# Moving VectorE work out of a crowded stage, and score steps later, in a fused retention and feed-forward kernel

## The chip, the cores and the metric

The kernel runs on one core of a Trainium2 chip. The metric is the time of one execution on the device in microseconds (us). The profile is one recorded execution. Its span leaves out some 1.7 us that the timed execution has around it, so spans are compared with spans and times with times. The profiled execution of the kernel before took 306.74 us, less than any of the timed ones beside it, so the gain is about 0.65 us smaller by the two profiled executions than by the medians.

The profile names the engines so: PE is TensorE (matmuls), DVE is VectorE, ACT is ScalarE, POOL is GpSimd, SP is SyncE; `SPq` and `ACTq` are DMA sends issued from SyncE's and ScalarE's queues.

## The reference, cut to what matters

```python
# q, k, v: [8 batches, 8 heads, 576 positions, 64], float32
scores = q @ k.T / sqrt(64)                       # per batch and head
ret    = scores * where(i >= j, gamma[h] ** (i - j), 0)
x      = (ret @ v)  -> [4608 tokens, 512]         # heads side by side
h      = x @ w_in                                 # 512 x 2048
g      = gelu_tanh(h)
out    = g @ w_out                                # 2048 x 512, float32
```

The decay mask can be factored over chunks of 128 positions. The kernel therefore works out scores within a chunk and carries a scanned state from chunk to chunk.

Of the kernel before, what the change touches and what calls it, by code (L numbers as in the profile page):

```python
# [19 lines left out]
def kernel(  # L20
# [9 lines left out]
    nc = tc.nc  # L30

    B, H, S, D = q.shape
    NT, DM = out.shape
    DF = moe_w_in.shape[1]
    HP = H // 2
    NC = S // 128
# [13 lines left out]
    NTB = NT // TB  # L50
# [121 lines left out]
    for u in range(2):  # L172
# [15 lines left out]
        out=cm, in_=cm, compare_op=ALU.is_ge, fill=0.0, base=0,  # L188
# [5 lines left out]
        out=tm, in_=tm, compare_op=ALU.is_ge, fill=0.0, base=0,  # L194
# [4 lines left out]
    for h in range(H):  # L199
        u = 64 * (h % 2)  # L200
# [78 lines left out]
    def turn(b, c, copy, tag="att"):  # L279
        a = att[b]  # L280
        t = bank(tag, "tr", F16)
        n = HP if c < NC else 2
        keys = "k" if b < NQ and c < NC else "kq"
        for y, key in enumerate(keys):
            for i in range(n):
                o = (512 * c if c < NC else 0) + 128 * i
                nc.tensor.transpose(
                    t[:, 128 * (n * y + i) : 128 * (n * y + i) + 128], act_of(b, key, c)[:, o : o + 128], ident
                )
        m = len(keys)  # L290
        d, o = turned(b, c)
        copy(
            out=d[:, 0:m, o : o + n, :].rearrange("p y n t -> p y (n t)"),
            in_=t[:, 0 : 128 * n * m].rearrange("p (y x) -> p y x", y=m),
        )
# [149 lines left out]
    def ost():  # L445
        return sb.tile([128, 2, DM], F32, tag="ost", name="ost", bufs=2)
# [17 lines left out]
    HD = DM // 2  # L464
# [4 lines left out]
    def weight_sums(f, names="1324"):  # L469
        s = slice(f, f + 4)  # L470
        w = {
            "1": (W12, W11, ALU.subtract), "3": (W22, W12, ALU.subtract),
            "2": (wt["3"], W11, ALU.add), "4": (W21, wt["2"], ALU.subtract),
        }
        for o in names:
            x, y, f = w[o]
            nc.vector.tensor_tensor(out=wt[o][:, s], in0=x[:, s], in1=y[:, s], op=f)  # L477
# [35 lines left out]
    keep = {}  # L513

    def after(t, m, u):
        last = t == NTB - 1
        if u == 0 and not (last and m in (6, 7, 4)):
            return
        us = slice(u, u + 1) if last and m in (6, 7, 4) else slice(0, 2)
        def pr(tag):  # L520
            return op[tag, u].rearrange("p (u d) -> p u d", u=2)
        def add(o, a, b):
            nc.vector.tensor_tensor(out=o, in0=a, in1=b, op=ALU.add)  # L523
        def send(o, i):
            if t < B:
                nc.sync.dma_start(
                    out=out[S * t : S * t + TB, :].rearrange("(u i p) d -> p u i d", u=2, i=2)[:, :, i, :], in_=o
                )
                return
            for v in range(2):  # L530
                end(o[:, v], i, v)
        def end(o, i, v, d=slice(0, DM)):
            b = 4 * v + 2 * i
            for h, e in enumerate((nc.sync, nc.scalar)):
                r0 = S * (b + h) + M0
                e.dma_start(out=out[r0 : r0 + TL, d], in_=o[TL * h : TL * h + TL, d])
        if m == 1:
            keep["s1"] = sb.tile([128, 2, HD], F32, tag="k1", name="k1", bufs=1)
            nc.scalar.copy(out=keep["s1"], in_=pr("A"))
        elif m == 6:  # L540
            if us.start == 0:
                keep["u2"] = sb.tile([128, 2, HD], F32, tag="k2", name="k2", bufs=1)
            add(keep["u2"][:, us], keep["s1"][:, us], pr("B")[:, us])
        elif m == 7:
            if us.start == 0:
                keep["u3"] = sb.tile([128, 2, HD], F32, tag="k3", name="k3", bufs=1)
            add(keep["u3"][:, us], keep["s1"][:, us], pr("B")[:, us])
            if u == 0:
                return
            keep["o1"] = ost()  # L550
            add(keep["o1"][:, :, HD:DM], keep["u3"], pr("C"))
            if last:
                for v in range(2):
                    end(keep["o1"][:, v], 1, v, slice(HD, DM))
        elif m == 2:
            keep["o0"] = ost()
            nc.scalar.copy(out=keep["o0"][:, :, 0:HD], in_=pr("A"))  # L557
        elif m == 3:
            add(keep["o0"][:, :, HD:DM], keep["u2"], pr("C"))
            send(keep["o0"], 0)  # L560
        elif m == 4:
            if last:
                add(keep["o1"][:, u, 0:HD], keep["s1"][:, u], pr("B")[:, u])
                end(keep["o1"][:, u], 1, u, slice(0, HD))
            else:
                add(keep["o1"][:, :, 0:HD], keep["s1"], pr("B"))
                send(keep["o1"], 1)
# [25 lines left out]
    V, P, A = nc.vector, nc.gpsimd, nc.scalar  # L593
# [48 lines left out]
    def at(t, u, f):  # L642
        if t > 0 and u > 29:
            t, u = t + 1, u - 30
        events.setdefault((t, u), []).append(f)
# [11 lines left out]
    at(0, 1, lambda: (new_casts(1), new_turned(1)))  # L657
    for p in range(HP):
        at(0, 2 + p, lambda p=p: cc(1, "q", p, V))
    at(0, 27, lambda: weight_sums(0, "32"))  # L660
    at(1, 4, lambda: weight_sums(0, "1"))
    at(1, 8, lambda: weight_sums(0, "4"))
    for p in range(HP):
        at(0, (20, 21, 22, 24)[p], lambda p=p: turn_q4(1, p, A.copy))
    CU = [(0, 6), (0, 27), (0, 31), (1, 0)]
# [6 lines left out]
        at(*VU[c], lambda c=c: (av(1, c, "AB"[c] if c < 2 else "att"), inter(1, c), put(1, c), spread(1, c, A.copy)))  # L672
    for c in range(NC):
        at(*SU[c], lambda c=c: (score(1, c), state(1, c), scan(1, c)))
    at(1, 10, lambda: weight_sums(4, "32"))
    at(1, 18, lambda: weight_sums(4, "1"))
    at(1, 24, lambda: weight_sums(4, "4"))


    def scores(t, u, *xs):  # L680
        at(t, u, lambda: [score(*x) for x in xs])
# [15 lines left out]
    def values(t, u, *xs):  # L697
        at(t, u, lambda: ([av(*x) for x in xs], [inter(*x[:2]) for x in xs]))
        for n, x in enumerate(xs):
            at(t, u + 1 + n, lambda x=x: put(*x[:2]))  # L700
# [5 lines left out]
        at(k[0], k[1] + 3, go)  # L706

    def turns_of(t, u, b, c, tag):
        at(t, u, lambda: turn(b, c, V.tensor_copy, tag))

    for b, (l, k, v) in TAILS.items():
        if b == 0:
# [6 lines left out]
    for t in range(1, 7):  # L719
        b, e = t + 1, t - 3  # L720
        if t == 1:
            for c, (u, tag) in enumerate(((7, "t2"), (9, "A"), (15, "C"), (17, "hp"))):
                turns_of(t, u, b, c, tag)
            u0, u1, u2, u3 = 11, 17, 19, 25
            states(t, u0, b, 0, "B")
            scores(t, u0, (b, 0, ("t0", "t1")), (b, 1, ("t2", "A")))
        else:
            u0, u1, u2, u3 = (8, 14, 19, 25) if t == 2 else (6, 12, 17, 24)
            tail = [(e, NC, ("B", "C"))] if e >= 0 else []
            scores(t, u0, (b, 0, ("t0", "t1")), (b, 1, ("t2", "A" if t > 2 else "C")), *tail)  # L730
        states(t, u1, b, 2, "t0")
        values(t, u1, (b, 0, "t1"), (b, 1, "t2"), *([(e, NC, "B")] if e >= 0 else []))
        scores(t, u2, (b, 2, ("t1", "t2")), (b, 3, ("hp", "hp")))
        if t < 6:
            states(t, u3, b + 1, 0, "t0")
        values(t, u3, (b, 2, "t1"), (b, 3, "t2"))
# [26 lines left out]
    for t in range(NTB):  # L763
        steps = []
        if t == 0:
            tags = ("A", "B", "C", "hp")
            for i0, f0, f1 in ((0, 0, 12), (2, 0, 8), (0, 12, 16), (2, 8, 16)):
                for f in range(f0, f1):
                    steps.append(lambda f=f, i0=i0: [down_mm(0, i0 + n, f, tags[i0 + n]) for n in range(2)] and None)
                if f1 == NF:  # L770
                    steps.append(lambda i0=i0: store_pair(0, i0))
        else:
            for u in range(2 if t == 1 else 0):
                for f in (0, NH, 2, NH + 2, 4, NH + 4, 6, NH + 6):
                    def half(u=u, f=f):
                        up_half(t, u, f)
                        if f in (NH + 2, NH + 6):
                            return lambda: act_sums(t, f - NH - 2, f - NH + 2, slice(u, u + 1))
                    steps.append(half)
            for f in range(0 if t == 1 else NH):  # L780
                steps.append(lambda f=f: up(t, f))
                def hi(f=f):
                    up(t, f + NH)
                    if f % 2:
                        return lambda: act_sums(t, f - 1, f + 1)
                steps.append(hi)
            for m in (1, 6, 5, 7, 2, 3, 4):
                for u in range(2):
                    steps.append(lambda m=m, u=u: (prod(t, m, u), after(t, m, u)))
        for u, s in enumerate(steps):  # L790
            then = s()
            run(t, u)
            if callable(then):
                then()
# [31 lines left out]
```

## The kernel before: the parts that the change touches

The tokens are done in nine blocks of 512 (`t` = 0 to 8). A block has a first layer of 16 steps `up` (four matmuls and a gelu each; in blocks 0 and 1 a step is eight matmuls of half width and a gelu, in an order of their own) and a second layer. The attention of batch t+1 is laid into the steps of block t, each piece at a fixed place: `at(t, u, f)` puts the work `f` into block t after step u. Block 0 counts its steps from the start of its second layer.

From block 1 on the second layer is done with seven half-size products in place of eight (a Strassen-like scheme). It needs sums of weight quarters, made once, and sums of gelu outputs, made in every block, both on VectorE. Each product fills one PSUM bank, A, B or C, and the bank must be copied or added away before the next product that uses it:

```python
def weight_sums(f, names="1324"):                 # one 128x1024 addition each
    ...
    for o in names:
        nc.vector.tensor_tensor(out=wt[o][:, s], in0=x[:, s], in1=y[:, s], op=f)

def act_sums(t, f0, f1, us=slice(0, 2)):          # four additions on VectorE: s1, s2, in place, s4
    ...
tag = {1: "A", 2: "A", 3: "C", 4: "B", 5: "C", 6: "B", 7: "B"}[m]     # bank of product m
...
for m in (1, 6, 5, 7, 2, 3, 4):                   # order of the products, two steps each
    for u in range(2):
        steps.append(lambda m=m, u=u: (prod(t, m, u), after(t, m, u)))
```

Batch 2 is transposed on TensorE and copied out of PSUM (`turn`); later batches are transposed by DMA, and TensorE meets the result in its scores. The steps at which a batch's scores, states and values stand:

```python
def turns_of(t, u, b, c, tag):
    at(t, u, lambda: turn(b, c, V.tensor_copy, tag))        # the copy is on VectorE
...
u0, u1, u2, u3 = (8, 14, 19, 25) if t == 2 else (6, 12, 17, 24)
scores(t, u0, ...first pair of chunks...)                   # masks "ret" on VectorE
states(t, u1, b, 2, "t0")                                   # then four spreads on ScalarE, at u1+2 to u1+5
values(t, u1, ...)                                          # xT copies on ScalarE, at u1+1 and u1+2
scores(t, u2, ...second pair...)
states(t, u3, b + 1, 0, "t0")                               # four spreads, at u3+2 to u3+5
values(t, u3, ...)
```

Steps 0 to 15 of blocks 2 and later are the first layer, 16 to 29 the products. A step past 29 runs on into the next block: with u3 = 25 the fourth spread, at u3+5, stands after step 0 of the next block.

## Time and profile before

| | before |
|---|---|
| time, median of the 4 runs beside the first run of the change | 307.39 us (307.03 to 307.96) |
| span of the profiled execution | 305.0 us |
| TensorE busy | 292.2 us, 96% |
| VectorE busy, whole span | 177.4 us, 58% |
| slices of VectorE from 61 to 84 us | 9, 9, 9 tenths |
| product stages of blocks 1 and 6 start | 73.92 us, 230.41 us |
| start of the last matmul to end | 4.96 us |

TensorE bounds the kernel, so the only question is where TensorE waits, and how long. Block 1 is the exception: there VectorE has no room, and TensorE waits for it.

### The profile page before, as it was taken

Reading aid. Unit: us, or ns where it says so; the run is one execution under the profiler, and the core shown is the slowest. Engines: PE = TensorE matmul, PEld = TensorE weight load, DVE = VectorE, ACT = ScalarE, POOL = GpSimd, SP = SyncE. Lnnn points to the kernel's source line nnn. Section 1 sums busy time; section 2 is a strip of 40 time slices with the busy share of each in tenths; the row PEclk is TensorE's granted clock in tenths of the full one; section 3 lists DMA queues with packets and bytes.
Section 4 is the critical chain, followed back from the end, with each engine's and each line's share of the span. In section 5 each row is a group of like instructions: output and inputs, shape, how many; then the busy total and the mean of one; then the engine's idle time right before and its main releaser. Section 6 shows DMA issues by size and latency. Waiting matters only on the chain.

```text
span 305.0 us, 6861 instructions
## 1 busy us (share of the span) xinstructions
PE 292.2 (96%) x2747; PEld 198.4 (65%) x2747; DVE 177.4 (58%) x362; ACT 168.5 (55%) x327; POOL 120.8 (40%) x178
## 2 busy tenths in 40 slices
PE   6899999999899999999999999999999899999993
PEld 2568655788784588457845785578557754784583
DVE  6652757699962865386538653865396335342432
ACT  6666417976556583659355936493647246316600
POOL 8679114560835069204920393039757110000000
PEclk9999999999999999999999999999999999999999
DMA  8999999999999995999399959963962140103004
GB/s 210 219 331 384 384 243 222 210 256 243 215 184 225 202 259 92 199 206 284 69 218 202 263 31 232 221 150 52 236 132 55 33 156 11 26 17 122 2 0 138
DMA packets 130591, 52.87 MB, mean 173 GB/s; under 512 B 118784, under 2 KB 121344, under 8 KB 130560
## 3 DMA queue, kind: packets, MB, share of 16 engines
q1 hardware_dynamic: 128544, 48.77, 74.0%
q0 software_dynamic: 1536, 3.15, 4.5%
q10 hardware_dynamic: 480, 0.52, 0.6%
q8 instruction: 21, 0.34, 0.5%
q14 instruction: 10, 0.08, 0.1%
HBM read 36.70 MB, written 9.44 MB: 151 GB/s over the span
## 4 chain that ended last, share of the span: by engine, by line
PE 66%; DVE 13%; ACT 5%; DMA 5%; SPq 5%; POOL 3%; issue 2%; DVEq 0%; POOLq 0%
PE hp L415 28%; PE opB L508 9%; PE hp L432 6%; PE opC L508 6%; PE opA L508 5%; PE op L451 4%; DVE ret L324 4%; SPq L95 3%; DMA tt<-cq 3%; ACT gT L421 2%; PE xs L367 2%; DMA ld<-in_moe_w_in_dram 2%; PE st L317 2%; PE xs L388 2%; DVE wt L477 1%
## 5 line engine op out<-in xcount | busy, mean ns | idle before, releaser
L415 PE MATMUL hp<-xT,w_in_sb 128*128 128x512 f16 x448 | 100.6, 379 | 0.1
L421 ACT ACTIVATE gT<-hp 128x512 f16<-128x512 f32 x112 | 66.9, 598 | 50.9 <-PE hp L415 44.0
L415 PEld LDWEIGHTS <-w_in_sb 128*128 128x128 f16 x448 | 42.9, 98 | 50.0 <-issue 2.0
L508 PEld LDWEIGHTS <-gT 128*128 128x128 f16 x512 | 49.8, 98 | 9.8 <-issue 2.6
L324 DVE TENSOR_TENSOR ret<-st,cm 128x512 f16<-128x512 f32 x64 | 40.0, 682 | 9.5 <-PE st L317 8.5
L488 DVE TENSOR_TENSOR s<-gT 128x512 f16<-128x512 f16 x32 | 14.0, 438 | 49.6 <-ACT gT L421 49.6
L257 POOL TENSOR_TENSOR ck<-ld,sc 128x512 f16<-128x512 f32 x31 | 32.8, 1059 | 23.4 <-DMA ld<-in_k_dram 22.2
L508 PEld LDWEIGHTS <-s 128*128 128x128 f16 x384 | 37.2, 98 | 6.0 <-issue 0.7
L508 PE MATMUL opA<-w_out_sb,gT 128*128 128x256 f16 x256 | 31.2, 273 | 0.6 <-DVE ret L324 0.6
L508 PE MATMUL opB<-wt,gT 128*128 128x256 f16 x256 | 30.6, 273 | 1.2 <-DVE k L523 0.8
L432 PE MATMUL hp<-xT,w_in_sb 128*128 128x256 f16 x256 | 29.8, 273 | 0.3 <-POOL w_in_sb L580 0.2
L557 ACT COPY ost<-opA 128x512 f32<-128x512 f32 x8 | 4.7, 585 | 46.0 <-PE opA L508 38.6
L752 POOL COPY gate<-s 128x1 f16<-128x1 f16 x5 | 0.9, 188 | 65.9 <-DVE s L491 57.4
L257 POOL TENSOR_TENSOR cq<-ld,sc 128x512 f16<-128x512 f32 x24 | 26.3, 1097 | 1.6 <-DMA ld<-in_q_dram 1.4
L432 PEld LDWEIGHTS <-w_in_sb 128*128 128x128 f16 x256 | 24.5, 98 | 3.7 <-POOL w_in_sb L580 0.4
L438 ACT ACTIVATE gT<-hp 128x512 f16<-128x512 f32 x32 | 19.1, 597 | 7.3 <-PE hp L432 7.3
L359 ACT CAST tbd<-ws 64x256 f16<-64x256 f32 x48 | 19.3, 402 | 2.9 <-DVE ws L354 2.2
L523 DVE TENSOR_TENSOR k<-k,opB 128x512 f32<-128x512 f32 (+1 forms) x18 | 11.3, 625 | 16.2 <-PE opB L508 14.8
L405 ACT CAST xT<-xs 128x512 f16<-128x512 f32 x32 | 18.5, 583 | 2.5 <-PE xs L388 2.1
L523 DVE TENSOR_TENSOR ost<-k,opC 128x512 f32<-128x512 f32 x16 | 11.0, 687 | 14.3 <-PE opC L508 14.0
L508 PE MATMUL opC<-wt,s 128*128 128x256 f16 x128 | 15.5, 273 | 0.6 <-DVE wt L477 0.6
L244 ACT CAST cv<-ld 128x512 f16<-128x512 f32 x27 | 15.7, 616 | 0.3
(95 smaller groups left out, 366.8 us busy)
## 6 DMA issues: line engine op xcount, KB each, us to landing
ld<-in_q_dram SPq DMA_DIRECT2D x32, 256.0 KB, 5.1
ld<-in_k_dram SPq DMA_DIRECT2D x32, 256.0 KB, 5.1
ld<-in_v_dram SPq DMA_DIRECT2D x32, 256.0 KB, 5.0
out_dram<-ost SPq DMA_DIRECT2D x16, 512.0 KB, 5.0
ld<-in_moe_w_in_dram SPq DMA_DIRECT2D x16, 256.0 KB, 5.6
ld<-in_moe_w_out_dram SPq DMA_DIRECT2D x16, 256.0 KB, 6.0
lt<-in_k_dram POOLq DMA_DIRECT2D x16, 64.0 KB, 4.6
lt<-in_q_dram POOLq DMA_DIRECT2D x16, 64.0 KB, 4.5
```

Source lines behind the costliest of these rows:

```text
L244: eng.copy(out=dst, in_=raw)
L257: eng.tensor_tensor(out=dst.rearrange("p (h d) -> p h d", d=D), in0=raw.rearrange("p (h d) -> p h d", d=D), in1=sc[:, s0 : s0 + nh].unsque ...
L324: nc.vector.tensor_tensor(out=r, in0=st[hl][:, 0:w], in1=m.rearrange("p n i -> p (n i)"), op=ALU.mult)
L359: cp(out=(tbd[b % 2][r, c, :, r] if c < NC - 1 else tbt[b % 4][r, :, r]), in_=att[b]["w", c][r])
L405: nc.scalar.copy(out=xT[:, g0 : g0 + 2], in_=src)
L415: nc.tensor.matmul(hp.rearrange("p (g t) -> p g t", t=TL), w_in_sb[:, ct, 128 * fc : 128 * fc + 128], xT[:, o : o + TB // TL, ct, :], star ...
L421: nc.scalar.activation(out=gT[t][:, fc].rearrange("p i n -> p (i n)"), in_=hp, func=AF.Gelu_apprx_tanh)
L432: nc.tensor.matmul(hp[:, 256 * x : 256 * x + 256].rearrange("p (g t) -> p g t", t=TL), w_in_sb[:, ct, 128 * (f + x) : 128 * (f + x) + 128] ...
L438: nc.scalar.activation(out=gT[t][:, f : f + 2, 2 * u : 2 * u + 2, :].rearrange("p f i n -> p f (i n)"), in_=hp.rearrange("p (f n) -> p f n ...
L488: nc.vector.tensor_tensor(out=s["1"], in0=a21, in1=a22, op=ALU.add)
L508: nc.tensor.matmul(op[tag, u][:, HD * u : HD * u + HD], lhs(f), rhs[:, f], start=(new and (u == 0 or own) and f == 0), stop=(f == NH - 1), ...
L523: nc.vector.tensor_tensor(out=o, in0=a, in1=b, op=ALU.add)
```

## The change

The intent has four parts. The first takes weight sums off VectorE in block 1, where it is full, and makes six of the eight in block 0. The second gives ScalarE the copies of batch 2's transposes. The third sets the second pair's scores behind product 6 (step 19 for 17), so that the masks no longer delay the addition that frees bank B, and exchanges banks to suit; in block 3 it also moves the first scores and states by a step, and in blocks 3 to 6 it moves the second values and the next batch's first states from step 24 to 25. The fourth changes the last block's product order, so that the large output sends leave earlier.

```diff
-    at(0, 27, lambda: weight_sums(0, "32"))
-    at(1, 4, lambda: weight_sums(0, "1"))
-    at(1, 8, lambda: weight_sums(0, "4"))
+    for t, u, f, n in ((0, 21, 0, "32"), (0, 22, 4, "3"), (0, 24, 4, "2"), (0, 27, 0, "1"), (0, 28, 4, "1"),
+                       (1, 20, 0, "4"), (1, 24, 4, "4")):
+        at(t, u, lambda f=f, n=n: weight_sums(f, n))
...
-    at(1, 10, lambda: weight_sums(4, "32"))
-    at(1, 18, lambda: weight_sums(4, "1"))
-    at(1, 24, lambda: weight_sums(4, "4"))
...
-        at(t, u, lambda: turn(b, c, V.tensor_copy, tag))
+        at(t, u, lambda: turn(b, c, A.copy, tag))
...
-            u0, u1, u2, u3 = (8, 14, 19, 25) if t == 2 else (6, 12, 17, 24)
+            u0, u1, u2, u3 = (8, 14, 19, 25) if t == 2 else (7, 13, 19, 25) if t == 3 else (6, 12, 19, 25)
...
-        values(t, u1, (b, 0, "t1"), (b, 1, "t2"), *([(e, NC, "B")] if e >= 0 else []))
-        scores(t, u2, (b, 2, ("t1", "t2")), (b, 3, ("hp", "hp")))
+        values(t, u1, (b, 0, "t1"), (b, 1, "t2"), *([(e, NC, "C")] if e >= 0 else []))
+        scores(t, u2, (b, 2, ("hp", "hp")), (b, 3, ("t1", "t2")))
...
-            for m in (1, 6, 5, 7, 2, 3, 4):
+            for m in (1, 6, 5, 7, 2, 3, 4) if t < NTB - 1 else (1, 6, 5, 2, 3, 7, 4):
```

Cut here: in the last block product 5's bank is copied out by ScalarE, and the right half of the output is added and sent per half, to go with the new order.

More of the change, by code (lines that the diff above doesn't have):

```diff
@@ L547, in after @@
             add(keep["u3"][:, us], keep["s1"][:, us], pr("B")[:, us])
-            if u == 0:
+            if last:
+                add(keep["o1"][:, u, HD:DM], keep["u3"][:, u], keep["o1"][:, u, HD:DM])
+                end(keep["o1"][:, u], 1, u, slice(HD, DM))
                 return
@@ L551, in after @@
             add(keep["o1"][:, :, HD:DM], keep["u3"], pr("C"))
-            if last:
-                for v in range(2):
-                    end(keep["o1"][:, v], 1, v, slice(HD, DM))
+        elif m == 5 and last:
+            keep["o1"] = ost()
+            nc.scalar.copy(out=keep["o1"][:, :, HD:DM], in_=pr("C"))
         elif m == 2:
```

## The prediction

> **What bounds the kernel now.** I read the page first (busy shares and slices), then who TensorE waited for, then TensorE's timeline, then the chain that ended last, then the groups by tile.
>
> ```profile
> PE 292.2 (96%) x2747; PEld 198.4 (65%) x2747; DVE 177.4 (58%) x362; ACT 168.5 (55%) x327; POOL 120.8 (40%) x178
> ...
> DVE  6652757699962865386538653865396335342432
> ```
>
> TensorE (PE) is busy in 96% of the span and its clock is full throughout. VectorE (DVE) is at 58% over the whole, but its row of slices reads 9, 9, 9 from about 61 to 84 us: block 1 is a stage with another limit. What can be won is TensorE's waiting, and that is little:
>
> ```profile
> engine line waited for: us in total, times, longest us
> ...
> PE opB L508 <- DVE k L523: 0.8, 1, 0.8
> ...
> PE opC L508 <- DVE wt L477: 0.6, 1, 0.6
> PE st L317 <- ACT xT L405: 0.6, 1, 0.6
> PE opA L508 <- DVE ret L324: 0.6, 1, 0.6
> PE st L317 <- DMA tt<-cq: 0.5, 1, 0.5
> ```
>
> This view understates waits, since it drops short ones and counts from the modelled end of a matmul. I therefore take starts in the timeline. A 128x256 matmul is issued every 0.109 us in steady state (sixteen in 1.745 us), a 128x512 one every 0.216 us; a start that comes later than that pace is a wait. Block 6, the worst:
>
> ```profile
> 230.41 1.91 PE L508 MATMUL opA<-w_out_sb,gT 128*128 128x256 f16 x16
> 232.25 0.62 PE L317 MATMUL st<-tt 64*128 64x128 f16 x16
> 233.03 1.91 PE L508 MATMUL opB<-wt,s 128*128 128x256 f16 x16 [0.15 <-ACT xT L398]
> 234.77 1.91 PE L508 MATMUL opC<-wt,s 128*128 128x256 f16 x16
> 237.52 1.91 PE L508 MATMUL opB<-wt,gT 128*128 128x256 f16 x16 [0.84 <-DVE k L523]
> ```
>
> The second opB (product 7) should start at 234.77 + 1.745 = 236.51 and starts at 237.52: 1.00 us lost. Scores to first opB (product 6) takes 0.78 us where block 2, without the bank conflict, takes 0.55: 0.23 more. The chain that ended last says why:
>
> ```profile
> 231.67 0.50 ACT gT L421
> ...
> 232.20 0.45 DVE s L488
> ...
> 232.67 0.72 DVE s L489
> ...
> 235.00 1.87 DVE ret L324 x3
> 236.87 0.60 DVE k L523
> ```
>
> Four masked score copies ("ret", 0.6 us each) stand on VectorE ahead of the addition "k" that frees bank B for product 7. Blocks 3, 4 and 5 show the same with 0.22 + 0.28 = 0.50 us each.
>
> **What the Trainium skill says.** (1) "Perfetto Trace Analysis", Identifying the Most-Contended Engine: matmul busy share is no measure of TensorE's headroom, as matmuls are pipelined; Optimization Strategy: look for the gaps and what ends them. The trace agrees: the groups show 273 ns a matmul where starts are 109 ns apart, so 96% busy alone tells nothing of what is left. (2) "ScalarE: Activation LUTs", What ACT_TABLE_LOAD costs: 0.833 ns per element over a fixed part, back-to-back overlap 93 ns. The trace agrees: 372 ns for 256 elements out of PSUM and 585 for 512 is 0.832 ns per element. (3) "SBUF — State Buffer", two separate sides: VectorE operations with two SBUF inputs and GpSimd exclude each other for a whole instruction. The trace agrees: a weight sum takes 0.68 us alone and 1.53 us at 80.0 us, while GpSimd (POOL) works without a pause.
>
> **The change, part by part.**
>
> *Weight sums.* Each is a 128x1024 addition on VectorE. Of the eight, six now run in block 0 and two in block 1. In block 0 VectorE idles 2.3 us before its copy at 46.5 and 1.3 us before the scores at 48.5; the three or four additions that move ahead of that (0.69 each) fit there. Two that sat before the scans at 50.0 are replaced by two others, so nothing shifts. Block 1 loses 0.60 + 0.60 + 1.55 + 1.54 us of VectorE time before 81.6 us. The last weight sum, needed only by product 4, stays.
>
> *Turned copies.*
>
> ```profile
> L292 ACT COPY tt<-tr x8: 577/586/593, 10.2 to 57.1; 128x512 f16<-128x512 f16 x8
> L292 DVE COPY tt<-tr x4: 678/684/685, 65.1 to 77.3; 128x1024 f16<-128x1024 f16 x4
> ```
>
> VectorE loses four of 0.60 net = 2.4 us. ScalarE (ACT) gains four of 1024 elements: 585 + 512 x 0.832 = 1.01 us, 0.92 net; an estimate from the trace's slope.
>
> Block 1 then goes so. Wait one, bank A for product 1, was at 73.14 and cost 0.72 us: VectorE ended the masks at 73.87. Now it is idle when the scans become ready at 68.7; scans 1.3 and four masks 2.4 end at 72.5, before TensorE arrives at 73.2: all 0.72 is gained. Wait three, product 5 for its weight sum, 0.73 us, goes too: that sum is made in block 0. Wait two, the second pair's scores for a bank that a ScalarE copy frees, cost 0.75 us. Here I walk ScalarE's new order from its gelu at 73.55: gelu to 74.15, turned copy to 75.05, two spreads to 75.75, copy of product 1 to 76.3, turned copy to 77.2, cast to 77.75, first output copy to 78.25, spread, second output copy to 79.2. TensorE reaches the scores at 78.25; the first score now goes to the hp banks and is done at 78.5, the last waits until 79.25. Still 0.7 us of waiting, but it ends 0.64 us earlier than at 79.89 now, and eight score matmuls less come after it. Together the block's product 5 runs about 1.6 us earlier.
>
> *Second pair's scores later (19 for 17), tail values in bank C for B.* In blocks 3 to 6 the addition "k" now precedes the masks on VectorE, as in block 2, which shows no wait. But product 6 now follows product 1 directly, with no scores between, and its seventh matmul reads activation sums of the last gelu pair. In block 4 the product stage starts at 168.91; those sums are ready at 171.58, plus 0.06, that is 2.73 after it; the matmul comes up at 1.745 + 6 x 0.109 = 2.40. A wait of 0.33 us takes the place of 0.50: 0.17 gained in block 4, the same in 5. In block 6 the sums ended at 233.39, 3.04 after the start, so 0.64 stays of 1.23: 0.59. In block 3 the earlier steps also move by one, which takes a spread and an output copy from before the last gelu; the sums come some 0.5 us earlier, no wait: 0.50 gained.
>
> *Block 3's scores at step 7 for 6.* The wait for the transposed queries cost 0.68 us (start 128.33 for 127.64). One step is four matmuls, 0.865 us: hidden, with 0.2 us in hand. 0.68 gained.
>
> *Last block.* No TensorE wait is there after 271 us, so the new product order saves none. The end does change:
>
> ```profile
> 296.32 5.46 SPq L536 DMA_DIRECT2D out_dram<-ost  x6
> ...
> 299.41 2.69 ACTq L536 DMA_DIRECT2D out_dram<-ost  x4
> 300.39 0.42 DVE L523 TENSOR_TENSOR ost<-k,opB 128x256 f32<-128x256 f32 x1 [0.45 <-PE opB L508]
> ```
>
> Four issues stand in ScalarE's queue from 299.41 to 302.1, so the last starts at 301.54 though its data is there at 300.81; SyncE's last starts at 301.24. In the new order the large sends go two products earlier, and each of the last four sums has one issue (0.55) per queue per 0.87 us. The last issue starts at about 300.9: 0.6 us gained. The landing (2.3 us) stays.
>
> **Sum.** 1.6 (block 1) + 0.68 + 0.50 (block 3) + 0.17 + 0.17 + 0.59 (blocks 4 to 6) + 0.6 (end) = 4.3 us. 307.28 - 4.3 = 303.0.
>
> **Rivals.** (a) *Every wait goes.* If the activation sums in blocks 4 to 6 come in time after all, blocks 4 to 6 give 2.2 and block 1 gives 2.2: with 1.2 and 0.6, 6.2 us, 301.1 us, just at the 2% line (301.13). For it: block 2 has the new order and no wait. Against: block 2 has no tail work on ScalarE ahead of its last gelu. (b) *ScalarE becomes block 1's bound.* It has about 6.0 us busy in the 8 us from 62 to 70; two copies bring 7.8. The first copies fit between gelus by my walk with under 0.1 us to spare; if not, or if turned copies hold up the output copies more, 1 to 1.5 us of the block's gain goes: about 304.2. For it: two gaps of only 0.27 us between gelus there. Against: TensorE's inserted transposes give 0.44 us more slack each. (c) *The gain is held up by loads.* The DMA engines are above 90% in most slices up to 110 us, and block 2's casts run when block 1's sums are done. If data came last, block 1's 1.6 us would reappear as a wait in block 2 or 3: about 304.5. Against: the last load of that batch was issued at 77.1 to 78.1 and lands about 5 us later, its cast is at 85.4, so 2 us are in hand.
>
> **Range and chances.** The sum is 4.3; (b) or (c) takes 1 to 1.6 off, (a) adds up to 1.9. So 301.6 to 304.5. To pass 2% needs practically every wait removed: 6%. Slower by 2% would need a new wait of 10 us: 1%.
>
> **What would show it.** Right: no wait at product 1 and at product 5 in block 1, about 0.7 us left before its second scores, ending in a ScalarE xT copy; in blocks 4 to 6 a wait of 0.3 to 0.6 us inside product 6 on VectorE's s, and none before product 7; no tt wait in block 3; turned copies of about 1.0 us; last DMA issue some 0.1 us after the last addition. Wrong: hp matmuls waiting for gelus in block 1, block 2 longer than 30.1 us, or a new wait at product 3 or 4 or at the start of a block, where output copies now come one step later.

## The result

The median went from 307.39 us (307.03 to 307.96) to 304.49 us (304.18 to 304.84), four runs each: 2.90 us less where 4.3 were predicted. The ratio is 0.9904, 95% interval 0.9885 to 0.9923, so the time is the same within 2%. (Ratios here are the mean time of one kernel's runs over that of the other's of the same rounds, so not quite the ratio of the quoted medians.) The span went from 305.0 to 302.8 us. All outputs are right.

The page of the kernel after, busy us with share and count, and VectorE's row of 40 slices:

```profile
PE 291.9 (96%) x2747; PEld 197.4 (65%) x2747; DVE 175.9 (58%) x359; ACT 173.0 (57%) x332; POOL 120.2 (40%) x178
...
DVE  6650879678962866386547653855396435342423
```

TensorE's busy time hardly moved; VectorE's three full slices of block 1 are now 7, 8 and 9. Whom TensorE waited for, in us in total, times and the longest:

```profile
PE opB L508 <- DVE s L489: 0.8, 3, 0.5
...
PE st L317 <- DMA tt<-cq: 0.5, 1, 0.5
PE st L317 <- ACT xT L405: 0.5, 1, 0.5
```

The waits for VectorE's `k`, `wt` and `ret` are gone. The wait for an `xT` copy is the second scores' in block 1, as foreseen. The three waits for `s` are the ones foreseen in blocks 4 to 6. The wait for the DMA transpose `tt` is still there, but not in the same block. Block 6 after, in TensorE's timeline (start, us, then the instruction; in brackets the idle time before it):

```profile
228.61 1.91 PE L508 MATMUL opA<-w_out_sb,gT 128*128 128x256 f16 x16
230.35 0.82 PE L508 MATMUL opB<-wt,s 128*128 128x256 f16 x6
231.64 1.26 PE L508 MATMUL opB<-wt,s 128*128 128x256 f16 x10 [0.47 <-DVE s L489]
232.84 0.62 PE L317 MATMUL st<-tt 64*128 64x128 f16 x16
233.39 1.92 PE L508 MATMUL opC<-wt,s 128*128 128x256 f16 x16
235.15 1.91 PE L508 MATMUL opB<-wt,gT 128*128 128x256 f16 x16
```

Product 7, the second opB of the fence, starts 235.15 - 233.39 = 1.76 us after product 5: it waits no more. Product 6 instead stops after six matmuls. Its seventh is due at 230.35 + 6 x 0.109 = 231.00 and starts at 231.64: 0.64 lost. The chain that ended last agrees:

```profile
230.40 0.45 DVE s L488
...
230.87 0.73 DVE s L489
...
231.64 1.26 PE opB L508 x10
```

The turned copies, with minimum, median and maximum in ns over all twelve, are now on ScalarE:

```profile
L292 ACT COPY tt<-tr x12: 577/586/1043, 10.0 to 76.3; 128x512 f16<-128x512 f16 x8, 128x1024 f16<-128x1024 f16 x4
```

At the end of the kernel, the last addition and the last send of each queue:

```profile
298.30 0.42 DVE L523 TENSOR_TENSOR ost<-k,opB 128x256 f32<-128x256 f32 x1 [0.45 <-PE opB L508]
...
298.84 0.55 SPq L536 DMA_DIRECT2D out_dram<-ost  x1
...
299.71 0.47 ACTq L536 DMA_DIRECT2D out_dram<-ost  x1
```

SyncE sends 0.11 us after the addition ends (298.73), ScalarE only 0.98 after it.

Setting TensorE's stage starts of one trace against the other's gives a ledger, in us gained against the kernel before. The second column of results is the first experiment, a repeat of the changed kernel.

| stage | predicted | after | repeat |
|---|---|---|---|
| start and block 0 | 0 | 0.13 | 0.00 |
| block 1 | 1.6 | 1.45 | 1.45 |
| block 2 | 0 | 0 | 0 |
| block 3 | 1.18 | 1.08 | 1.08 |
| block 4 | 0.17 | -0.04 | -0.04 |
| block 5 | 0.17 | -0.62 | -0.26 |
| block 6 | 0.59 | 0.38 | 0.38 |
| block 7 | 0 | -0.29 | -0.28 |
| block 8 | 0 | 0 | 0 |
| last matmul to end | 0.6 | 0.20 | 0.38 |
| sum | 4.3 | 2.3 | 2.7 |

The ledger names the questions. Why do blocks 4, 5 and 6 fall short by about 0.2 each, and block 5 by more? What happens in block 7, which the change does not touch? What became of the end? And is it the weight sums or the copies that won block 1?

**Blocks 4 to 6, the common 0.2.** ScalarE at the start of block 6 after:

```profile
213.54 0.60 ACT L421 ACTIVATE gT<-hp 128x512 f16<-128x512 f32 x1 [2.42 <-PE hp L415]
214.16 0.40 ACT L359 CAST tbd<-ws 64x256 f16<-64x256 f32 x1
214.59 1.26 ACT L421 ACTIVATE gT<-hp 128x512 f16<-128x512 f32 x2
```

A spread (`tbd`) stands between the block's first and second gelu. It is the fourth spread of u3, which u3 = 25 puts after step 0 of the next block. The second gelu is held up. There are two `hp` banks, so TensorE's fourth step needs the one that this gelu frees: it ends at 215.19, while the step's first matmul was due 0.216 us after the one at 214.83, at 215.05. It comes 0.19 us late. The same 0.186 to 0.188 us stands after the matmuls at 152.67, 183.46 and 214.83, so in blocks 4, 5 and 6. It stood already in the trace before, at 93.69 and 123.80, the starts of blocks 2 and 3, which follow the two blocks that had u3 = 25.

**Block 5, the rest.** TensorE waits for the transposed queries:

```profile
187.99 0.62 PE L317 MATMUL st<-tt 64*128 64x128 f16 x16 [0.51 <-DMA tt<-cq]
```

The matmul before it starts at 187.10. Where nothing is waited for, a first score starts 0.31 us after the matmul before it (in blocks 2, 4 and 7 of all twelve traces), so this one was due at 187.41, and 0.58 us is lost. In the trace before this wait had only just been missed: the transpose landed at 189.69, and the matmul before the scores made room for them at 189.74.

**Block 7.** The first gelu's wait ends at 244.32 in the trace, and it starts at 244.65 with nothing visible in between. TensorE's third step, which needs the bank that it frees, then comes 0.31 us late, after the matmul at 244.77. This gelu is the 320th instruction that the trace has of ScalarE in all six traces with the copies there, and the 316th in the six without. A cause that goes by the place in ScalarE's program, as the fetching of instructions might, would fit; no run tests it.

### The profile page after: what moved, and what is told of

It is laid out like the page before. It is cut to its first block, busy times and chain, and to the rows that moved or that the text cites. A ratio compares the mean times of both kernels' runs of the same rounds, so it can differ in the third digit from the quotient of the medians.

```text
span 302.8 us, 6867 instructions
## 1 busy us (share of the span) xinstructions
PE 291.9 (96%) x2747; PEld 197.4 (65%) x2747; DVE 175.9 (58%) x359; ACT 173.0 (57%) x332; POOL 120.2 (40%) x178
## 4 chain that ended last, share of the span: by engine, by line
PE 74%; ACT 9%; DMA 5%; SPq 4%; POOL 3%; issue 2%; DVE 1%; POOLq 0%
PE hp L415 28%; PE opB L508 11%; PE opC L508 8%; PE hp L432 7%; PE opA L508 6%; PE op L451 4%; SPq L95 3%; DMA tt<-cq 3%; PE st L317 3%; PE xs L367 2%; ACT gT L421 2%; DMA ld<-in_moe_w_in_dram 2%; PE xs L388 2%; ACT xT L405 1%; PE us L338 1%
## 5 line engine op out<-in xcount | busy, mean ns | idle before, releaser
L488 DVE TENSOR_TENSOR s<-gT 128x512 f16<-128x512 f16 x32 | 14.7, 458 | 50.0 <-ACT gT L421 49.0
L508 PEld LDWEIGHTS <-s 128*128 128x128 f16 x384 | 36.5, 98 | 6.2 <-DVE s L489 1.6
L257 POOL TENSOR_TENSOR cq<-ld,sc 128x512 f16<-128x512 f32 x24 | 25.2, 1052 | 2.6 <-DMA ld<-in_q_dram 2.5
L523 DVE TENSOR_TENSOR ost<-k,opC 128x512 f32<-128x512 f32 x15 | 10.3, 687 | 16.4 <-PE opC L508 16.1
L508 PE MATMUL opB<-wt,s 128*128 128x256 f16 x128 | 15.8, 273 | 0.8 <-DVE s L489 0.8
```

What stands on the lines that cost most here:

```text
L257: eng.tensor_tensor(out=dst.rearrange("p (h d) -> p h d", d=D), in0=raw.rearrange("p (h d) -> p h d", d=D), in1=sc[:, s0 : s0 + nh].unsque ...
L488: nc.vector.tensor_tensor(out=s["1"], in0=a21, in1=a22, op=ALU.add)
L508: nc.tensor.matmul(op[tag, u][:, HD * u : HD * u + HD], lhs(f), rhs[:, f], start=(new and (u == 0 or own) and f == 0), stop=(f == NH - 1), ...
L523: nc.vector.tensor_tensor(out=o, in0=a, in1=b, op=ALU.add)
```

## The experiments

The theory: the gains are the waits named, block by block; the shortfall is the spread behind u3 = 25 (3 x 0.19), the transposes' landing in block 5, and a send that waits at the end. The rivals: ScalarE is made the bound of block 1 by the turned copies; and chance from run to run makes up the rest.

Runs of one group share the runs of the kernel before: 307.79 us (11 runs) for the first four, 307.50 (7) for the next four, 307.87 (7) for the last two.

### a_again: the changed kernel once more, five rounds

> The changed kernel once more, unchanged. Question: is the 0.68 us wait for the transposed queries in block 5 chance or systematic? Theory: chance. In both traces TensorE reaches those scores 17.4 us after the gate copy on GpSimd, and the transposes land 16.5 to 17.9 us after it, so a wait of 0 to 0.6 us falls on any of blocks 4, 5 and 6, in either kernel. Expected: 304.0 to 304.8 us, a tt wait in another block or none, with block 5's gain back where it is none. Rival: the change moves TensorE ahead of the transposes; then block 5 waits 0.5 to 0.7 us again. Both: gelu waits of 0.19 us at the third to fourth hp matmul group of blocks 4, 5 and 6, waits on s of 0.17, 0.17 and 0.47, and a last ScalarE issue that starts about 0.9 us after the last addition, as the lane of its semaphore is that of the second large send.

Measured: 304.24 us (303.92 to 305.09), ratio 0.9884 (0.9861 to 0.9906), span 302.3. In medians that is 3.55 us less than the kernel before, where the first run of the change had 2.90. The ledger above has its trace beside the first. The three gelu waits (0.186 each), the three `s` waits (0.33, 0.33, 0.64), block 1 and block 7 came back to within 0.01 us. The `tt` wait in block 5 was 0.22 for 0.58 and the end 0.38 for 0.20. So the wait was in block 5 again, where the expectation was another block or none. The rival does not hold either: p_wts, which leaves these steps as they were, has 0.55 us of it in block 5. So between these two executions only the start and the two terms that hang on DMA landings differ, by 0.1 to 0.4 us each; the rest of the ledger is the program's.

### p_wts: the kernel before with the weight sums moved, nothing else

```diff
-    at(0, 27, lambda: weight_sums(0, "32"))
-    at(1, 4, lambda: weight_sums(0, "1"))
...
+    for t, u, f, n in ((0, 21, 0, "32"), (0, 22, 4, "3"), (0, 24, 4, "2"), (0, 27, 0, "1"), (0, 28, 4, "1"),
+                       (1, 20, 0, "4"), (1, 24, 4, "4")):
...
```

> The kernel before with the weight sums moved alone. Theory (the two VectorE reliefs of block 1 are redundant, and the copies on ScalarE cost something): the wait at product 1 and the wait at product 5 both go, and since ScalarE has no turned copies its output copies come earlier, so block 1 from its first product to the start of block 2 gains 1.5 to 2.0 us; the rest as before: 305.3 to 305.9 us. Rival (both reliefs are needed): less than 1.0 us gained in block 1, with a ret wait of 0.3 us or more left at product 1.

Measured: 305.08 us (304.94 to 305.66), ratio 0.9909 (0.9883 to 0.9935), span 303.4. Block 1 gained 2.06 us, just over what was expected and more than the 1.45 of the whole change. No wait is left at products 1 and 5, and the second scores wait only 0.16 us. The sums alone are therefore enough for block 1.

### p_turn: the kernel before with the turned copies on ScalarE, nothing else

```diff
-        at(t, u, lambda: turn(b, c, V.tensor_copy, tag))
+        at(t, u, lambda: turn(b, c, A.copy, tag))
```

> The kernel before with batch 2's turned copies on ScalarE alone. Theory: VectorE is relieved of 2.4 us, which takes away the wait at product 1 (0.72) in whole or nearly; product 5's weight sum, still on VectorE behind the scans, is done some 1.2 to 2 us earlier, so its wait of 0.73 goes too or falls below 0.3; about 0.7 us of waiting for the ScalarE output copy stays at the second scores. Block 1 gains 1.0 to 1.5 us: 305.8 to 306.4 us. Rival (VectorE is still the bound without moving the sums): a wt wait of 0.5 us or more stays at product 5 and block 1 gains under 0.8.

Measured: 306.58 us (306.31 to 308.14), ratio 0.9965 (0.9934 to 0.9996), span 306.4. Block 1 gained only 0.61, so the rival held. Product 1 still waits 0.66 us for `ret`, product 5 still waits 0.63 for `wt`; and block 3 waits 1.85 us for `tt`, in a profiled execution that was the slowest of the four by 1.5 us. Where did VectorE's freed time go? Its groups between 61 and 74.5 us (count, then busy us, mean ns, idle us), first before:

```profile
L477 DVE TENSOR_TENSOR wt<-w_out_sb 128x1024 f16<-128x1024 f16 x2 | 1.6, 806 | 0.0
L488 DVE TENSOR_TENSOR s<-gT 128x512 f16<-128x512 f16 x3 | 1.5, 495 | 0.0
```

and in this run:

```profile
L477 DVE TENSOR_TENSOR wt<-w_out_sb 128x1024 f16<-128x1024 f16 x2 | 2.2, 1104 | 0.0
L488 DVE TENSOR_TENSOR s<-gT 128x512 f16<-128x512 f16 x3 | 2.0, 674 | 0.0
```

Two copies, 1.2 us net, left this window, and the same five additions took 0.6 + 0.5 = 1.1 us longer. All of it is in two of the five. Each of these two reads two SBUF inputs and starts while a GpSimd operation is running, by the trace's spans, which are rough on GpSimd. In both traces the smaller one ends 0.28 us after that operation has ended (66.66 after 66.37 here, 66.32 after 66.04 before) and the larger one 0.55 us after it (69.84 after 69.29, 69.50 after 68.95). They took longer here because more of the GpSimd operation was still to come when they started. This fits the exclusion that the prediction cites. That GpSimd is the cause was not tested by itself: no run here took GpSimd's work away.

### a_noturn: the changed kernel with the turned copies back on VectorE

```diff
-        at(t, u, lambda: turn(b, c, A.copy, tag))
+        at(t, u, lambda: turn(b, c, V.tensor_copy, tag))
```

> The changed kernel with batch 2's turned copies back on VectorE. Theory: with the weight sums in block 0 VectorE has room for them, and ScalarE's output copies come 0.4 to 0.8 us earlier; the wait at the second scores of block 1 falls from 0.67 to 0.0 to 0.3 us, no wait returns at product 1 or 5: 0.3 to 0.6 us faster than the changed kernel. Rival (VectorE becomes the bound again): a ret wait at product 1 or a later scan brings the wait to 0.6 us or more, and the kernel is no faster or slower by up to 0.7 us.

Measured: 303.57 us (302.58 to 303.77), ratio 0.9848 (0.9821 to 0.9875), against 304.24 (303.92 to 305.09) for the changed kernel on the same chip; the two ranges do not meet. Block 1 gained 2.22 us for 1.45. The second scores in block 1, first with the copies on ScalarE (the changed kernel):

```profile
78.32 0.45 PE L317 MATMUL st<-tt 64*128 64x128 f16 x9
79.27 0.38 PE L317 MATMUL st<-tt 64*128 64x128 f16 x7 [0.50 <-ACT xT L405]
79.58 1.92 PE L508 MATMUL opC<-wt,s 128*128 128x256 f16 x16
```

and in this run:

```profile
78.99 0.62 PE L317 MATMUL st<-tt 64*128 64x128 f16 x16
79.54 1.92 PE L508 MATMUL opC<-wt,s 128*128 128x256 f16 x16
```

With the copies on ScalarE the sixteen scores stop after nine, for a bank that a ScalarE copy frees; with the copies on VectorE they run through. So part two of the change costs 0.77 us in block 1 once part one is in. Block 7's 0.29 was gone too. Over all twelve profiled executions, that wait is in each of the six with the copies on ScalarE and in none of the six without (the kernel before among these). The copies end at 77 us and block 7 begins 166 us later, so what ties them is open.

### p_late: the kernel before with the score steps and banks moved, nothing else

```diff
-            u0, u1, u2, u3 = ... (6, 12, 17, 24)
+            u0, u1, u2, u3 = ... (7, 13, 19, 25) if t == 3 else (6, 12, 19, 25)
...
-        scores(t, u2, (b, 2, ("t1", "t2")), (b, 3, ("hp", "hp")))
+        scores(t, u2, (b, 2, ("hp", "hp")), (b, 3, ("t1", "t2")))
(and bank "C" for "B" in the tail's values)
```

> The kernel before with the later second scores, the tail values in bank C and the hp banks for the first of the second pair alone. Theory: block 3 gains 1.0 to 1.2 us (no tt wait, no wait at products 6 and 7); blocks 4 and 5 gain nearly nothing each (0.50 of waits gone, 0.33 new at product 6's seventh matmul on s, 0.19 new at the next block's second gelu), block 6 gains 0.3 to 0.5; block 1 and the end as before. Together 1.2 to 1.7 us less a wait of up to 0.7 for transposes in one of blocks 4 to 6: 305.6 to 306.6 us. Rival (what block 1 gained is needed first, later waits only take over): under 0.7 us in all.

Measured: 305.88 us (305.38 to 306.83), ratio 0.9960 (0.9928 to 0.9993), span 304.3. Block 3 gained 1.07, block 4 -0.03, block 5 -0.04, block 6 0.38, block 7 0. There was no `tt` wait. With the landings out of the picture the sum can be checked: block 4 won 0.50, paid back 0.33 to `s` and 0.19 to the gelu, which is -0.02. The change's own gain in blocks 4 and 5 is nothing.

### p_last: the kernel before with the last block's order changed, nothing else

```diff
-            for m in (1, 6, 5, 7, 2, 3, 4):
+            for m in (1, 6, 5, 7, 2, 3, 4) if t < NTB - 1 else (1, 6, 5, 2, 3, 7, 4):
(and the copy, additions and sends that go with it)
```

> The kernel before with the last block's product order and split sums alone. Theory: no TensorE time changes; from the last matmul to the end of the span 4.95 us become 4.5 to 4.8, as SyncE's last issue follows the last addition by 0.1 us but ScalarE's waits until the second large send of its queue has landed, 0.8 to 1.0 us after that addition. Rival (my prediction: only the issue queue counts): both last issues within 0.2 us of the last addition and 4.35 us to the end.

Measured: 308.17 us (307.26 to 308.29), ratio 1.0025 (1.0001 to 1.0050), span 306.4. The stage that it changes got shorter: last matmul to end took 4.64 us for 4.96. SyncE's last send started 0.10 us after the last addition, ScalarE's 0.88 after it. The profiled execution lost 1.1 us in block 1, where its program is the same as before: VectorE additions there took 1.15 to 1.53 us, and TensorE waited 1.14 us for a turned copy. Whether the other three runs lost it there too can't be seen from their times, so in the total this run settles nothing; for the end of the kernel its trace says the same as the changed kernel's.

### a_u24: the changed kernel with u3 = 24 again

```diff
-            u0, u1, u2, u3 = ... (7, 13, 19, 25) if t == 3 else (6, 12, 19, 25)
+            u0, u1, u2, u3 = ... (7, 13, 19, 24) if t == 3 else (6, 12, 19, 24)
```

> The changed kernel with the second values of blocks 3 to 6 and the next batch's first states back at step 24 (from 25). Theory: the fourth spread is then queued on ScalarE before the next block's first gelu, as in the kernel before, so the gelu waits of 0.19 us at the starts of blocks 4, 5 and 6 go: 0.5 to 0.6 us less than the changed kernel, nothing new elsewhere. Rival (the values now wait for masks that come later since the scores did): a ret wait of 0.2 us or more at step 24 in each of these blocks, and no gain.

Measured: 304.41 us (304.06 to 304.53), ratio 0.9908 (0.9887 to 0.9928), span 302.7. ScalarE at the start of block 6:

```profile
213.11 0.60 ACT L421 ACTIVATE gT<-hp 128x512 f16<-128x512 f32 x1 [1.31 <-PE hp L415]
213.91 0.60 ACT L421 ACTIVATE gT<-hp 128x512 f16<-128x512 f32 x1 [0.21 <-PE hp L415]
```

No spread stands between the gelus, and all three gelu waits of blocks 4 to 6 are gone, with no new wait at step 24. The cause of the 3 x 0.19 is thereby shown. The time did not follow: a `tt` wait of 0.60 us fell on block 6 in the profiled execution and ate what was won. As a way to a faster kernel the run is inconclusive.

### a_tail: the changed kernel with eight sends at the end in place of twelve

```diff
                 add(keep["o1"][:, u, HD:DM], keep["u3"][:, u], keep["o1"][:, u, HD:DM])
-                end(keep["o1"][:, u], 1, u, slice(HD, DM))
                 return
...
-                end(keep["o1"][:, u], 1, u, slice(0, HD))
+                end(keep["o1"][:, u], 1, u)
```

> The changed kernel with the second row blocks of the end sent as whole rows after product 4, so with 8 sends at the end in place of 12. Theory (a semaphore lane is used again after eight sends, and the last ScalarE send waits for the landing of the large one on its lane): with no lane used twice both last issues start within 0.3 us of the last addition, and the end comes 0.1 to 0.4 us sooner, the larger pieces (128 KB) taking back some. Rival (the ScalarE queue is slow for another reason): its last issue still starts 0.6 us or more after the addition.

The theory here was that ScalarE's last send waits for a semaphore, which the ninth and later sends share with earlier ones. In the changed kernel it starts at 299.71, just after 299.64, when ScalarE's second send, four sends before it and on the same semaphore in the trace, has landed; in p_last the same pair is 303.36 and 303.28. Measured: 305.11 us (304.87 to 305.31), ratio 0.9932 (0.9912 to 0.9952), span 303.2. The last addition ends at 299.01, and the last send of ScalarE is

```profile
299.05 0.52 ACTq L536 DMA_DIRECT2D out_dram<-ost  x1
```

0.04 us after it: the wait is gone, as the theory said. But the last two sends now carry whole rows, 128 KB for 64, and landed at 301.84, and addition to end took 4.15 us where the changed kernel takes 4.03. The wait was real, and taking it away this way is worth nothing.

### a_713: the changed kernel with block 3's early steps in all later blocks, and u3 = 24

```diff
-            u0, u1, u2, u3 = ... (7, 13, 19, 25) if t == 3 else (6, 12, 19, 25)
+            u0, u1, u2, u3 = ... (7, 13, 19, 24)
```

> The changed kernel with blocks 4 to 6 on block 3's steps (first scores 7, first values 13), and the second values of blocks 3 to 6 at step 24. Theory: one step more hides the landing of the transposes (16.5 to 17.9 us after the gate copy; TensorE comes at 18.1 to 18.3 in place of 17.4), so no tt wait in blocks 4 to 6; the last gelu pair is no longer behind a spread and an output copy, so no wait on s inside product 6 (0.33, 0.33, 0.64 now), as in block 3; no gelu wait at block starts (0.19 each). Together 1.7 to 2.4 us less than the changed kernel: 302.0 to 302.9 us. Rival: the waits take each other's place, so that 1.0 us or less is gained, with a new wait at product 5 for the tail's copy out of bank C.

Measured: 303.60 us (303.11 to 305.84, 5 runs), ratio 0.9852 (0.9827 to 0.9877), so less was gained than expected. The profiled execution is the slow one of the five: it lost some 3 us before block 1, at the loads of the first weights, so its span (304.1) is not to be compared. From block 1 to the last matmul it gained 3.57 us on the kernel before, where the changed kernel gained 1.95. In blocks 4 to 6 there is no gelu wait, no `s` wait in blocks 4 and 5, 0.52 left in block 6, and at `tt` 0.13 us, in block 5. TensorE comes to the scores 18.14 us after the copy that lets the casts begin, where it came after 17.39 in the changed kernel, so the transposes have 0.75 us more to land.

### best: a_713 with the turned copies on VectorE

```diff
-        at(t, u, lambda: turn(b, c, A.copy, tag))
+        at(t, u, lambda: turn(b, c, V.tensor_copy, tag))
...
-            u0, u1, u2, u3 = ... (7, 13, 19, 25) if t == 3 else (6, 12, 19, 25)
+            u0, u1, u2, u3 = ... (7, 13, 19, 24)
```

> The same as a_713 with batch 2's turned copies on VectorE, meant to beat both kernels. Theory: the two gains add, as they lie in different blocks: 0.7 less in block 1 than a_713 and no 0.3 us wait at the start of block 7: 301.2 to 302.2 us, 5.5 to 6.5 us less than the kernel before. Rival: block 1's gain is used up by a later wait on the transposes in block 3, whose slack falls to 1 us or less: 302.3 us or more.

Measured: 302.22 us (301.82 to 302.43), ratio 0.9815 (0.9794 to 0.9836), span 300.7. It beats both kernels: 5.65 us less than the kernel before in medians, where the change gave 2.90 and 3.55. Against the 2% line the run stays unclear, as its interval has 0.98 inside. Its median is just at the upper end of what was expected. The view of TensorE's waits, which drops short ones, leaves these beyond block 0's casts and transposes:

```profile
PE hp L432 <- POOL w_in_sb L582: 1.1, 2, 0.7
...
PE opB L508 <- DVE s L489: 0.4, 1, 0.4
```

One is at the start, for the weights' loads, and one is in block 6, 0.52 us by starts. By starts there are also 0.19 us at the beginning of blocks 2 and 3, where the u3 = 25 of blocks 1 and 2 was left as it is, 0.19 in block 7 and 0.30 in block 1.

## Why the prediction was right, and where its steps were not

The range held, with luck: 304.49 lies 0.01 us under the upper end of 301.6 to 304.5, one of the four runs lies over it, and the centre of 303.0 was 1.5 us too low. The repeat's 304.24 lies inside. By its steps:

- **Weight sums, waits one and three of block 1: right.** No wait is left at products 1 and 5, in the changed kernel or in p_wts alone.
- **Turned copies, wait two: right in size, wrong in sign of its worth.** The walk through ScalarE's order said that about 0.7 us stays before the second scores; 0.70 was measured, and the second output copy ended at 79.22 for the 79.2 of the walk. The copy itself took 1.00 to 1.04 us for the 1.01 estimated. But the prediction counted this part as a help to VectorE, and a_noturn shows that it takes 0.77 us from block 1 after the sums have moved. Rival (b), ScalarE as block 1's bound, was thus half true inside a term that came out right: 1.6 predicted, 1.45 measured, 2.22 to be had. And p_turn shows that, in the window looked at, relief by the copies alone is nearly all lost on VectorE.
- **Scores after product 6: right in mechanism.** The `s` waits were predicted as 0.33, 0.33 and 0.64 and measured as 0.33, 0.33 and 0.64, with none before product 7 and none in block 3. The failed step is what the same line of the diff also does: u3 went from 24 to 25, and the spread at u3+5 crossed into the next block. The prediction asked whether a new wait would come "at the start of a block" and put no number on it, though the trace before had 0.19 us of it after both blocks with u3 = 25. That is 3 x 0.19 = 0.56 us of the shortfall, shown by a_u24.
- **Block 3's step: right, one term read 0.09 us too large.** 0.68 + 0.50 = 1.18 predicted, 1.08 measured, and no `tt` wait there in either run of the changed kernel. The prediction took the first score to be due 0.216 us after the matmul before it, but it comes 0.31 us after it where nothing is waited for. The wait was 0.59 us, not 0.68, and that is the difference.
- **Block 5's transposes: not seen.** The slack there was 0.05 us in the trace before, and it was not looked at. TensorE reaches these scores 17.35 to 17.39 us after the copy that lets the casts begin, in blocks 5 and 6, before and after (17.20 in a_u24); over the twelve traces the transposes land 16.0 to 18.2 us after it. How long the wait is, up to 0.6 us, is chance; where it falls is less so. Of the ten traces with these scores at step 6, six wait in block 5 (0.22 to 0.58), one in block 6 (a_u24), none in block 4. Block 3 has one too: 0.59 before, 0.64 in p_last, 1.85 in p_turn. Moving the scores a step later, as in block 3, is the cure: 0.13 is left in a_713, none in best. Why block 5's landing is the latest of the three, 17.0 to 18.2 us in all traces but a_u24 (16.6), stays open.
- **The end: the term was mis-sized.** 0.6 was predicted, 0.20 and 0.38 measured, 0.32 in p_last. The step "last issue some 0.1 us after the last addition" holds for SyncE (0.11) and fails for ScalarE (0.98): its last send waits for an earlier one to land. a_tail confirms the wait, and shows that less waiting did not bring an earlier end with larger pieces.
- **Block 7: not seen and not explained.** 0.3 us, tied to the copies on ScalarE by twelve executions, without a cause that a run shows.

The gap of the first trace is thus accounted for: 0.21, 0.79 and 0.21 us in blocks 4, 5 and 6 (0.56 of it the gelu waits, most of the rest the transposes), 0.29 in block 7, 0.40 at the end, and 0.25 in blocks 1 and 3, less 0.13 that the start gained, make the 2.0 between 4.3 and 2.3. Rival (c), a load that holds up block 2 or 3, did not happen: block 2 lost nothing.

## What to carry to other kernels

Work out what a changed step number does to *every* instruction that is placed relative to it, up to the first instruction of the next stage; a wait of the same kind elsewhere in the trace before gives its price. When two parts of a change relieve the same engine, test each alone, since the second may only load another engine with what the first has made room for. Where a transfer lands within a tenth of a us of its use, count the length of the wait as a matter of luck, and look for a schedule that gives it room.

## What the Trainium skill lacked or had wrong

- "Perfetto Trace Analysis", section Optimizing Scalar/DVE Operations, says that with a saturated DVE "offloading some work to Scalar (or even GPSIMD) may make sense". It lacks the test whether DVE is still the limit: four copies moved to ScalarE gave 0.61 us in block 1 by themselves (p_turn), and cost 0.77 us when DVE's load had already been moved away (a_noturn against the changed kernel).
- "SBUF — State Buffer", two separate sides, has the exclusion of VectorE's two-SBUF-input operations and GpSimd, which agrees with the trace (0.68 against 1.53 us for one weight sum). It does not warn that taking other VectorE work away can bring more such meetings: in p_turn 1.1 of the 1.2 us taken away came back as longer additions, if that exclusion is what lengthened them; each of the two ended 0.28 or 0.55 us after the GpSimd operation that it met.
- "DMA: Bandwidth & Descriptors", section Anatomy of one DMA, says that a semaphore wait takes place on the issuing sequencer before dispatch. This agrees with the trace, which has the wait in ScalarE's own program (over at 299.68, the send at 299.71), but the page does not say what it can cost when two sends of a queue share a semaphore: 0.98 us (the changed kernel) and 0.88 us (p_last) from data to send with twelve sends, 0.04 us with eight (a_tail).
- No page gives the spread of a DMA transpose's landing from one execution to the next: here 16.0 to 18.2 us after the same starting copy in blocks 5 and 6, which put waits of 0.2 to 0.6 us into one or the other.
- No page that I read names the cause of the gelu of block 7 that starts 0.33 us after its last visible wait ended, in six of six executions with four more ScalarE copies in block 1 and in none of six without.
